# Wider rows for the key and value caches: four heads interleaved on a tile's partitions, in a fused decode kernel

## The chip, the cores and the metric

The kernel runs on one core of a Trainium2 chip. The metric is the device time of one execution in microseconds (us). The time before is 137.99 us, the median of 3 runs (137.91 to 138.05). A profile is one execution taken by the hardware profiler; its span (first to last instruction) is about 2 us shorter than the time.

Engines: PE is TensorE's matmuls, PEld its weight loads, DVE is VectorE, ACT is ScalarE, SPq is the queue of SyncE, which issues the transfers. PSUM is the memory that PE writes its results to. The granted clock is the share of its full speed that TensorE was given at that time, as the profile lists it. L291 means line 291 of that run's kernel; the same statement has another number in another kernel.

## The reference, cut to what matters

One decode step: an attention over the last 4,096 positions of a cache, beside a small GELU MLP, mixed by a sigmoid gate. All data is bf16.

```python
# x (1,1,576); 32 query heads on 16 KV heads of 128; window W = 4096
g = sigmoid((x * gate_w).sum(-1, keepdims=True))
q = x @ wq                                     # wq 576 x 4096
k, v = k_cache[:, :, -4096:], v_cache[:, :, -4096:]   # 16 heads x 4096 x 128, 16 MiB each
p = softmax(q k^T / sqrt(128)) ;  a = (p v) @ wo      # wo 4096 x 576
b = gelu(x @ w1 + b1) @ w2 + b2                # w1 576 x 4608, w2 4608 x 576
out = g * a + (1 - g) * b                      # (1,1,576)
```

Nearly everything is reading: 53.61 MB of weights and cache for one row of output. The scores are so small with these inputs that the attention is close to uniform. A kernel that pairs keys wrongly still passes the comparison.

## The kernel before

The stream of loads is w1, wq, K, V, wo, w2, all issued by SyncE. K and V come one head at a time, each head as 128 rows of 8 KB in one of eight buffers. DVE turns each K tile as 4-byte words (a word is two bf16; the code that follows takes them as turned by 32 x 32 blocks), and PE multiplies it by the query, spread out so that each 32-partition quarter gives its own rows of scores.

```python
k_t = kv_pool.tile([P, NCH * Dh], BF16, name="kv_t", tag="kv")       # 8 buffers, P = 128, NCH = 32
nc.sync.dma_start(out=k_t[:],
    in_=A_k_cache[0, h, Sk - W : Sk, :].rearrange("(p c) d -> p (c d)", p=P))
kt = early[:, (h % 2) * W : (h % 2 + 1) * W]
nc.vector.transpose(out=kt.bitcast(FP32), in_=k_t[:].bitcast(FP32))  # L291
kv = kt.rearrange("p (c b k t) -> p c b k t", c=NCH, b=2, t=2)
for j in range(4):
    for f in range(2):
        nc.tensor.matmul(s_ps[:, f * 512 : (f + 1) * 512].rearrange("p (c k) -> p c k", k=32),
            lhsT=qz[:, h, j, :], rhs=kv[:, f * 16 : (f + 1) * 16, j // 2, :, j % 2], ...)   # L295
# ... softmax: one exp over 128 x 1024; then V, per head, 32 matmuls into o_ps ...
# ... loads: wo in four pieces, then w2 in six ...
for r in range(RO): y_add(ov[:, r : r + 1], wo_t[:, r, :])            # y_add: 512 + 64 columns, one partition
for f in range(NF): y_add(gt[:, f : f + 1], w2_t[:, f, :], stop=(f == NF - 1))
nc.scalar.copy(out=out_row[:, 320:D], in_=y_ps[0:1, 320:D])
nc.vector.tensor_copy(out=out_row[:, 0:320], in_=y_ps[0:1, 0:320])
nc.sync.dma_start(out=out..., in_=out_row[:])
```

Note how PE reads the turned keys: `j % 2` takes every second bf16 of a run of adjacent words.

Of the kernel before, what the change touches and what calls it, by code (L numbers as in the profile page):

```python
# [8 lines left out]
FP32 = mybir.dt.float32  # L9
BF16 = mybir.dt.bfloat16  # L10
ACT = mybir.ActivationFunctionType
ALU = mybir.AluOpType
# [4 lines left out]
def kernel(  # L17
# [21 lines left out]
    NCH = W // P  # L39
# [4 lines left out]
    KM = 4  # L44
    DM = KM * P
    DL = D - DM
    QH = Hq * Dh // 2
    N0 = 512
# [4 lines left out]
    kv_pool = ctx.enter_context(tc.tile_pool(name="kv_pool", bufs=8, side="right"))  # L53
# [7 lines left out]
    x_row = const.tile([1, D], BF16, name="x_row")  # L61
    nc.scalar.dma_start(out=x_row[:], in_=A_x.rearrange("a b d -> (a b) d"))
    gw_row = const.tile([1, D], BF16, name="gw_row")
    nc.scalar.dma_start(out=gw_row[:], in_=gate_w.rearrange("(o n) -> o n", o=1))
    b2_row = const.tile([1, D], BF16, name="b2_row")
    nc.scalar.dma_start(out=b2_row[:], in_=B_b2.rearrange("(o n) -> o n", o=1))
    b1_row = const.tile([1, F], BF16, name="b1_row")
    nc.scalar.dma_start(out=b1_row[:], in_=B_b1.rearrange("(o n) -> o n", o=1))


    w1_t = big.tile([P, KM * F + FH], BF16, name="w1_t", tag="B")
    w1_m = w1_t[:, 0 : KM * F].rearrange("p (k n) -> p k n", k=KM)
    w1_l = w1_t[:, KM * F :]
    w1_src = B_w1[0:DM, :].rearrange("(p k) n -> p k n", k=KM)
    for k in range(KM):
        nc.sync.dma_start(out=w1_m[:, k, :], in_=w1_src[:, k, :])  # L76
    nc.sync.dma_start(out=w1_l, in_=B_w1[DM:D, :].rearrange("r (two n) -> (r two) n", two=2))

    wq_t = big.tile([P, KM * Hq * Dh + QH], BF16, name="wq_t", tag="A")
    wq_m = wq_t[:, 0 : KM * Hq * Dh].rearrange("p (k n) -> p k n", k=KM)  # L80
    wq_l = wq_t[:, KM * Hq * Dh :]
    wq_src = A_wq[0:DM, :].rearrange("(p k) n -> p k n", k=KM)
    for k in range(KM):
        nc.sync.dma_start(out=wq_m[:, k, :], in_=wq_src[:, k, :])
    nc.sync.dma_start(out=wq_l, in_=A_wq[DM:D, :].rearrange("r (two n) -> (r two) n", two=2))
# [4 lines left out]
    one_f = const.tile([1, P], FP32, name="one_f")  # L90
    nc.vector.memset(one_f[:], 1.0)
# [5 lines left out]
    nc.vector.reduce_sum(out=par[:], in_=ident_f[:].rearrange("p (a t) -> p t a", t=2), axis=AX.X)  # L97
    lo32 = const.tile([P, 32], FP32, name="lo32")
# [5 lines left out]
    same = const.tile([P, 4, 32], FP32, name="same")  # L104
    for b in range(4):
        nc.vector.tensor_copy(out=same[:, b, :], in_=lo32[:])

# [7 lines left out]
    early = big.tile([P, 2 * W + 8320], BF16, name="early", tag="C")  # L115
    qz_flat = early[:, 2 * W :]
    qz = qz_flat[:, 0 : Hkv * 4 * P].rearrange("p (h j m) -> p h j m", h=Hkv, j=4)


    xt_ps = ps_m.tile([P, 8], FP32, name="xt_ps", tag="m")  # L120
    for k in range(KM):
        nc.tensor.matmul(
            xt_ps[:, k : k + 1], lhsT=x_row[0:1, k:DM:KM], rhs=one_b[0:1, 0:1], start=True, stop=True
        )
    xd = const.tile([1, DL, 2], BF16, name="xd")
    for t in range(2):
        nc.vector.tensor_copy(out=xd[:, :, t], in_=x_row[0:1, DM:D])
    nc.tensor.matmul(
        xt_ps[:, 4:6],
        lhsT=xd[:].rearrange("p a t -> p (a t)"),  # L130
        rhs=one_b[0:1, 0:2],
        start=True,
        stop=True,
    )
    xt = const.tile([P, KM], BF16, name="xt")
    nc.vector.tensor_copy(out=xt[:], in_=xt_ps[:, 0:KM])
    xl = const.tile([P, 2], BF16, name="xl")
    nc.vector.tensor_tensor(out=xl[:], in0=xt_ps[:, 4:6], in1=par[:], op=ALU.mult)

    nc.vector.memset(qz_flat.bitcast(FP32), 0.0)  # L140

    junk_row = const.tile([1, D], BF16, name="junk_row")
    s0 = const.tile([1, 1], FP32, name="s0")
    nc.vector.tensor_tensor_reduce(
        out=junk_row[:],
        in0=x_row[:],
        in1=gw_row[:],
# [7 lines left out]
    nc.tensor.matmul(g_ps[:, 0:1], lhsT=one_f[0:1, 0:P], rhs=s0[0:1, 0:1], start=True, stop=True)  # L155
# [11 lines left out]
        out=b2g[:], in0=b2_row[:], scalar1=omg[0:1, 0:1], scalar2=None, op0=ALU.mult  # L167
# [3 lines left out]
    y_ps = ps_y.tile([1, 1024], FP32, name="y_ps")  # L171

    def y_add(vec, row, start=False, stop=False):
        nc.tensor.matmul(  # L174
            y_ps[0:1, 0:N0], lhsT=vec, rhs=row[:, 0:N0], start=start, stop=stop, skip_group_check=True
        )
        nc.tensor.matmul(  # L177
            y_ps[0:1, N0:D], lhsT=vec, rhs=row[:, N0:D], start=start, stop=stop, skip_group_check=True
        )

    y_add(one_f[0:1, 0:1], b2g[0:1, :], start=True)
# [3 lines left out]
    for c in range(NF):  # L185
        f0 = (c // NJ) * FH + c % NJ
        nc.tensor.matmul(  # L187
            h_ps[:, c : c + 1],
            lhsT=b1_row[0:1, f0 : (c // NJ + 1) * FH : NJ],
            rhs=one_b[0:1, 0:1],  # L190
            start=(c == 0),
            stop=False,
            skip_group_check=True,
        )
    for k in range(KM):
        for c in range(NF):
            f0 = (c // NJ) * FH + c % NJ
            nc.tensor.matmul(  # L198
                h_ps[:, c : c + 1],
                lhsT=w1_m[:, k, f0 : (c // NJ + 1) * FH : NJ],  # L200
                rhs=xt[:, k : k + 1],
                start=False,
                stop=False,
                skip_group_check=True,
            )
    for j in range(NJ):
        nc.tensor.matmul(  # L207
            h_ps[:, j:NF:NJ],
            lhsT=w1_l[:, j:FH:NJ],
            rhs=xl[:, 0:2],  # L210
            start=False,
            stop=(j == NJ - 1),
            skip_group_check=True,
        )
# [28 lines left out]
    for k in range(KM):  # L243
        for j in range(Hq):
            nc.tensor.matmul(  # L245
                q_ps[:, j : j + 1],
                lhsT=wq_m[:, k, j * Dh : (j + 1) * Dh],
                rhs=xt[:, k : k + 1],
                start=(k == 0 and j == 0),
                stop=False,  # L250
                skip_group_check=True,
            )
    for j in range(Hq // 2):
        nc.tensor.matmul(
            q_ps[:, j : Hq : Hq // 2],
            lhsT=wq_l[:, j * Dh : (j + 1) * Dh],
            rhs=xl[:, 0:2],
            start=False,
            stop=(j == Hq // 2 - 1),
            skip_group_check=True,  # L260
        )
# [11 lines left out]
    for b in range(4):  # L273
        rows = slice(32 * b, 32 * b + 32)
        diag = qz_flat[rows, 32 * b : 32 * b + Hkv * 514].rearrange("p (h m) -> p h m", m=514)
        eng = nc.vector.tensor_copy if b % 2 == 0 else nc.scalar.copy
        eng(
            out=diag[:, :, 0:512].rearrange("p h (j m) -> p h j m", m=P)[:, :, :, 0:2],
            in_=qj_ps[rows].rearrange("p j h t -> p h j t"),
        )  # L280


    s_ps = ps_s.tile([P, NCH * 32], FP32, name="s_ps")
    for h in range(Hkv):
        k_t = kv_pool.tile([P, NCH * Dh], BF16, name="kv_t", tag="kv")
        nc.sync.dma_start(
            out=k_t[:],
            in_=A_k_cache[0, h, Sk - W : Sk, :].rearrange("(p c) d -> p (c d)", p=P),
        )
        kt = early[:, (h % 2) * W : (h % 2 + 1) * W]  # L290
        nc.vector.transpose(out=kt.bitcast(FP32), in_=k_t[:].bitcast(FP32))  # L291
        kv = kt.rearrange("p (c b k t) -> p c b k t", c=NCH, b=2, t=2)
        for j in range(4):
            for f in range(2):
                nc.tensor.matmul(  # L295
                    s_ps[:, f * 512 : (f + 1) * 512].rearrange("p (c k) -> p c k", k=32),
                    lhsT=qz[:, h, j, :],
                    rhs=kv[:, f * 16 : (f + 1) * 16, j // 2, :, j % 2],
                    start=(h == 0 and j == 0),
                    stop=(h == Hkv - 1 and j == 3),  # L300
                    skip_group_check=True,
                )

# [5 lines left out]
    mh = const.tile([1, Hq], FP32, name="mh")  # L309
    nc.vector.reduce_max(out=mh[:], in_=mt_ps[:].rearrange("p (b h) -> p h b", b=4), axis=AX.X)  # L310
    mh4 = const.tile([1, 4, Hq], FP32, name="mh4")
    for b in range(4):
        nc.vector.tensor_copy(out=mh4[:, b, :], in_=mh[:])
# [22 lines left out]


    o_ps = ps_o.tile([P, Hq], FP32, name="o_ps")
    for h in range(Hkv):
        v_t = kv_pool.tile([P, NCH, Dh], BF16, name="kv_t", tag="kv")  # L340
        nc.sync.dma_start(
            out=v_t[:],
# [79 lines left out]
```

## Time and profile before

| what | before |
|---|---|
| time, span | 137.99 us, 136.1 us |
| K transposes on DVE | 16, mean 2,304 ns |
| score matmuls | 128; within a run one starts every 0.217 us (from the starts in the trace, granted clock 1.00) |
| last weight byte landed (from the packets in the trace) | 131.68 us |
| last matmul ended | 133.17 us |

The page of the profile: busy share of DVE, then of the DMA engines (tenths), and the rate moved, in 40 slices of 3.40 us each.

```profile
DVE  5873002228689999989974250000000030000001
...
DMA  4999999999999999999999999999999999999940
GB/s 122 423 425 421 420 419 419 408 420 412 421 421 424 419 417 421 419 417 424 419 421 414 419 421 424 412 421 412 417 421 414 427 427 406 433 417 426 403 182 0
```

The DMA row has no hole: the kernel is bound by its loads, at about 420 GB/s. But DVE's row is at 9 or 8 through the K stage, which is the second limit, close behind.

The groups of instructions (line, engine, operation, output and input with shapes, count, then busy us and mean ns of one, then the idle time just before them and who ended it):

```profile
L295 PE MATMUL s_ps<-early 128*128 128x512 bf16 x128 | 32.6, 401 | 10.5 <-DVE early L291 10.5
L291 DVE STREAM_TRANSPOSE early<-kv_t 128x2048 f32<-128x2048 f32 x16 | 36.6, 2304 | 3.6 <-DMA kv_t<-in_A_k_cache_dram 1.9
```

The chain that ended last, in order of time (start, us, what), only its end:

```profile
86.88 18.95 DMA kv_t<-in_A_v_cache_dram
105.85 22.70 DMA w_t<-in_B_w_dram
...
132.92 0.22 PE y_ps L174
133.13 0.04 PE y_ps L177
133.20 0.37 ACT out_row L389
133.60 0.48 DVE out_row L390
```

The last weights land, PE works off the rows of w2 that are left, and two copies run one after the other.

### The profile page before, as it was taken

How to read it: one execution, taken by the hardware profiler on the slowest of the kernel's cores; microseconds unless marked ns; L12 is line 12 of the kernel's file. 1: busy time of each engine (PE TensorE's matmuls, PEld its weight loads, DVE VectorE, ACT ScalarE, POOL GpSimd, SP SyncE). 2: the span in 40 equal slices, each digit the busy share in tenths (PEclk: the TensorE clock that was granted, in tenths of full speed). 3: DMA queues.
4: the chain of work that ended last, by engine and by line, in shares of the span. 5: the costliest groups of instructions: out<-in, count | busy, mean ns of one | idle time of the engine just before them, and what ended most of it. 6: DMA issues, size and time to landing. Idle time of an engine off the chain costs nothing.

```text
span 136.1 us, 2522 instructions
## 1 busy us (share of the span) xinstructions
PE 90.0 (66%) x1140; PEld 54.9 (40%) x1140; DVE 53.4 (39%) x83; ACT 3.8 (3%) x8; POOL 0.7 (1%) x6
## 2 busy tenths in 40 slices
PE   0099999352997978768774239453352459987891
PEld 0089599341342323323231239452342433433340
DVE  5873002228689999989974250000000030000001
ACT  3000000000000000000000300000000000000001
POOL 2000000000000000000000000000000000000000
PEclk9999999999999999999999655555555555799999
DMA  4999999999999999999999999999999999999940
GB/s 122 423 425 421 420 419 419 408 420 412 421 421 424 419 417 421 419 417 424 419 421 414 419 421 424 412 421 412 417 421 414 427 427 406 433 417 426 403 182 0
DMA packets 7509, 53.79 MB, mean 395 GB/s; under 512 B 837, under 2 KB 841, under 8 KB 1481
## 3 DMA queue, kind: packets, MB, share of 16 engines
q1 hardware_dynamic: 7490, 53.61, 95.6%
q8 instruction: 9, 0.15, 0.4%
q14 instruction: 2, 0.02, 0.0%
q10 hardware_dynamic: 8, 0.01, 0.0%
HBM read 53.62 MB, written 0.00 MB: 394 GB/s over the span
## 4 chain that ended last, share of the span: by engine, by line
DMA 77%; DVE 9%; PE 9%; issue 2%; SPq 1%; ACT 0%; DVEq 0%
DMA kv_t<-in_A_v_cache_dram 27%; DMA kv_t<-in_A_k_cache_dram 27%; DMA w_t<-in_B_w_dram 24%; DVE early L291 9%; PE s_ps L295 5%; PE y_ps L174 3%; PE o_ps L346 1%; SPq L76 1%; PE y_ps L177 0%; DVE out_row L390 0%; ACT out_row L389 0%; DVEq L291 0%
## 5 line engine op out<-in xcount | busy, mean ns | idle before, releaser
L295 PE MATMUL s_ps<-early 128*128 128x512 bf16 x128 | 32.6, 401 | 10.5 <-DVE early L291 10.5
L291 DVE STREAM_TRANSPOSE early<-kv_t 128x2048 f32<-128x2048 f32 x16 | 36.6, 2304 | 3.6 <-DMA kv_t<-in_A_k_cache_dram 1.9
L346 PE MATMUL o_ps<-pt,kv_t 128*128 128x2 bf16 x512 | 15.4, 165 | 16.2 <-DMA kv_t<-in_A_v_cache_dram 13.7
L295 PEld LDWEIGHTS <-early 128*128 128x128 bf16 x128 | 12.8, 100 | 29.9 <-issue 16.3
L346 PEld LDWEIGHTS <-kv_t 128*128 128x128 bf16 x512 | 14.8, 105 | 17.1 <-DMA kv_t<-in_A_v_cache_dram 14.5
L370 DVE COPY o_sb<-o_ps 128x32 f32<-128x32 f32 x1 | 0.2, 191 | 29.1 <-PE o_ps L346 29.1
L174 PE MATMUL y_ps<-wo_t,ov 128*1 128x512 bf16 x32 | 10.9, 471 | 0.6 <-DMA wo_t<-in_A_wo_dram 0.6
L174 PE MATMUL y_ps<-w_t,gt 128*1 128x512 bf16 x36 | 9.2, 379 | 1.8 <-DMA w_t<-in_B_w_dram 1.8
L390 DVE CAST out_row<-y_ps 1x320 bf16<-1x320 f32 x1 | 0.5, 478 | 22.8 <-ACT out_row L389 22.8
L198 PE MATMUL h_ps<-xt,w_t 128*128 128x1 bf16 x144 | 9.3, 201 | 0.0
L198 PEld LDWEIGHTS <-w_t 128*128 128x128 bf16 x144 | 9.1, 167 | 0.2 <-issue 0.2
L177 PE MATMUL y_ps<-wo_t,ov 128*1 128x64 bf16 x32 | 7.0, 218 | 0.0
L177 PE MATMUL y_ps<-w_t,gt 128*1 128x64 bf16 x36 | 6.9, 192 | 0.0
L174 PEld LDWEIGHTS <-ov 128*1 128x1 bf16 x32 | 3.2, 100 | 6.6 <-issue 3.8
L245 PE MATMUL q_ps<-xt,wq_t 128*128 128x1 bf16 x128 | 3.9, 165 | 2.3 <-DMA wq_t<-in_A_wq_dram 2.3
L174 PEld LDWEIGHTS <-gt 128*1 128x1 bf16 x36 | 3.0, 84 | 4.8
L245 PEld LDWEIGHTS <-wq_t 128*128 128x128 bf16 x128 | 3.7, 105 | 2.4 <-DMA wq_t<-in_A_wq_dram 2.4
L216 DVE COPY hacc<-h_ps 128x36 f32<-128x36 f32 x1 | 0.2, 195 | 11.1 <-PE h_ps L207 11.1
L177 PEld LDWEIGHTS <-gt 128*1 128x1 bf16 x36 | 3.0, 84 | 2.1 <-issue 2.1
L140 DVE MEMSET early<- 128x4160 f32 x1 | 3.5, 3525 | 0.8 <-issue 0.8
L177 PEld LDWEIGHTS <-ov 128*1 128x1 bf16 x32 | 3.0, 94 | 0.2 <-issue 0.2
L187 PE MATMUL h_ps<-one_b,b_row 1*128 1x1 bf16 x36 | 2.4, 196 | 0.3 <-DMA b_row<-in_B_b_dram 0.3
(75 smaller groups left out, 31.5 us busy)
## 6 DMA issues: line engine op xcount, KB each, us to landing
kv_t<-in_A_k_cache_dram SPq DMA_DIRECT2D x16, 1024.0 KB, 18.2
kv_t<-in_A_v_cache_dram SPq DMA_DIRECT2D x16, 1024.0 KB, 17.5
w_t<-in_B_w_dram SPq DMA_DIRECT2D x5, 1152.0 KB, 9.0
wo_t<-in_A_wo_dram SPq DMA_DIRECT2D x4, 1152.0 KB, 20.5
wq_t<-in_A_wq_dram SPq DMA_DIRECT2D x4, 1024.0 KB, 13.6
w_t<-in_B_w_dram SPq DMA_DIRECT2D x2, 1296.0 KB
w_t<-in_B_w_dram SPq DMA_DIRECT2D x1, 720.0 KB, 22.0
w_t<-in_B_w_dram SPq DMA_DIRECT2D x1, 576.0 KB
```

The lines of the kernel that those rows point to most:

```text
L76: nc.sync.dma_start(out=w1_m[:, k, :], in_=w1_src[:, k, :])
L140: nc.vector.memset(qz_flat.bitcast(FP32), 0.0)
L174: nc.tensor.matmul(y_ps[0:1, 0:N0], lhsT=vec, rhs=row[:, 0:N0], start=start, stop=stop, skip_group_check=True)
L177: nc.tensor.matmul(y_ps[0:1, N0:D], lhsT=vec, rhs=row[:, N0:D], start=start, stop=stop, skip_group_check=True)
L187: nc.tensor.matmul(h_ps[:, c : c + 1], lhsT=b1_row[0:1, f0 : (c // NJ + 1) * FH : NJ], rhs=one_b[0:1, 0:1], start=(c == 0), stop=False, sk ...
L198: nc.tensor.matmul(h_ps[:, c : c + 1], lhsT=w1_m[:, k, f0 : (c // NJ + 1) * FH : NJ], rhs=xt[:, k : k + 1], start=False, stop=False, skip_ ...
L216: nc.vector.tensor_copy(out=hacc[:], in_=h_ps[:])
L245: nc.tensor.matmul(q_ps[:, j : j + 1], lhsT=wq_m[:, k, j * Dh : (j + 1) * Dh], rhs=xt[:, k : k + 1], start=(k == 0 and j == 0), stop=False ...
L291: nc.vector.transpose(out=kt.bitcast(FP32), in_=k_t[:].bitcast(FP32))
L295: nc.tensor.matmul(s_ps[:, f * 512 : (f + 1) * 512].rearrange("p (c k) -> p c k", k=32), lhsT=qz[:, h, j, :], rhs=kv[:, f * 16 : (f + 1) * ...
L346: nc.tensor.matmul(o_ps[:, 2 * h : 2 * h + 2], lhsT=v_t[:, c, :], rhs=pt[:, c, 2 * h : 2 * h + 2], start=(c == 0), stop=(c == NCH - 1),)
L390: nc.vector.tensor_copy(out=out_row[:, 0:320], in_=y_ps[0:1, 0:320])
```

## The change

Intent: longer pieces per row in the loads, a shorter tail, and less work left when the last weights land.

1. K and V come four heads at a time. Partition 4k + b holds head b, key block k, so a partition's row is 32 KB and a whole group is 4 MB, in one of four large buffers which K, V, w2 and wo share. Loads are of 1 to 4 MB. w1 and wq also come in longer contiguous runs.
2. Because four heads are interleaved on the partitions, the turned words of the four heads are interleaved too. The transpose undoes that while it writes: it writes at a step of 8 words, so that each head's 8 words lie together.
3. The probabilities of the four heads must be kept apart. Each half of the scores is exponentiated four times, with a bias of -1e30 on the rows of the other heads ("masked exp copies").
4. Half of w2 is loaded and used between K and V instead of at the end.
5. The output row y sits on 2 partitions of PSUM (0 and 32, 288 columns each), so one copy replaces two.

```diff
-        nc.vector.transpose(out=kt.bitcast(FP32), in_=k_t[:].bitcast(FP32))
+    # head_rows: cache[0, 4g:4g+4, -W:].rearrange("b (k c) d -> k b (c d)", k=32)
+    for g in range(NG):                                   # 4 groups of 4 heads
+        k_t = big.tile([P, NCK, Dh], BF16, name="k_t", tag="CDBA"[g])
+        load(k_t, A_k_cache, g, k_cuts[g])
+        for f in range(2):
+            for u in range(2):
+                nc.vector.transpose(
+                    out=kt[...].bitcast(FP32).rearrange("p (n b k) -> p n k b", b=HB, k=8),
+                    in_=k_t[...].bitcast(FP32).rearrange("p (n k b) -> p n k b", b=HB, k=8))
+            kv = kt[:].rearrange("p (c e b k t) -> p c e b k t", e=2, b=HB, k=8, t=2)
+            # matmuls as before, rhs=kv[:, :, j // 2, b, :, j % 2]
...
+            nc.scalar.activation(out=p_t[:, cs, :, b], in_=s_ps[...], func=ACT.Exp,
+                bias=negm[:, b : b + 1], scale=SCALE, accum_out=...)      # b in 0..3, two halves
...
+    w2_t = big.tile([P, NF, D], BF16, name="w2_t", tag="B")   # the buffer of K's third group
+    nc.sync.dma_start(out=w2_t[:, 0:NJ, :], in_=w2_src[:, 0])
+    for f in range(NJ):
+        y_add(gt[:, f : f + 1], w2_t[:, f, :])
...
+    for g in range(NG):
+        v_t = big.tile([P, NCK, Dh], BF16, name="v_t", tag="CDAC"[g])   # the last reuses V's first
+        load(v_t, A_v_cache, g, v_cuts[g])
...
+        for s in range(2):                                  # y_add
+            nc.tensor.matmul(y_ps[32 * s : 32 * s + 1, :], lhsT=vec, rhs=row[:, s * DH : (s + 1) * DH], ...)
...
-    nc.scalar.copy(...) ; nc.vector.tensor_copy(...)
+    nc.vector.tensor_copy(out=out_row[0:33, :], in_=y_ps[0:33, :])
```

## The prediction

> **What bounds it now.** The slices show DMA at 0.99 from 2 to 131 us, about 420 GB/s, for 53.61 MB. The chain of waits is 77% DMA; PE is busy 66%, DVE 39%. After the last weight bytes come 36 output matmuls of w2 (0.245 us a row) ending at 133.17, two serial copies (0.36 and 0.48 us) and an output transfer of about 2 us: span 136.1, time 138.0. The K stage is close to a second limit: 16 transposes of 2.30 us against 2.5 us of DMA per MB.
>
> **What the change does.**
> 1. Longer rows. The trace's packets took 313 ns (8,192 B), 351 (9,216), 393 (10,368), 180 (4,608): an estimated 9.6 ns plus 27.0 bytes/ns. Data rows fall from 6,656 to 3,840, so 176 fewer per engine, 1.7 us; 22 fewer completion packets of 9 ns, 0.2 us. All on the critical path: about -1.9 us.
> 2. Tail. One copy of 288 columns replaces two serial ones: -0.4 us. With half of w2 gone from the end, w2's last 18 rows land within 6.3 us of wo's last 20; at 0.245 us a row PE needs 9.3 us and would end 3 us late. [...]
> 3. DVE. Transposes stay 16 x 2,048 fp32, but now write with a step of 8 words. [...]a reduction reading at a step of 32 words took 373 ns, a contiguous one 264, the same shape from PSUM 278: 0.7 to 0.85 ns more per element. For writes nothing here shows it. Estimate with the same penalty: 3.7 to 4.1 us each.
> 4. Middle. Four 4 MB buffers hold all of K; w2's first half waits for the third group's 12 transposes. They start near 30.5 us and K's stream ends near 65, so a transpose up to about 2.9 us is hidden. At 3.8 us w2 is issued near 76 and the queue runs dry for about 11 us. Eight masked exps (about 6 us of ACT instead of 1.1) hide behind w2 and V.
>
> **Sum.** Without the write penalty: -1.9 -0.4 -0.7 = about 135 us. With it: 142 to 150. I hold the unpenalised case somewhat likelier: putting w2 ahead of V would be odd if DVE lagged far.
>
> Predicted 135.8 us, 8 in 10 between 133.3 and 148. Faster by over 2%: 0.36; within 2%: 0.25; slower: 0.39.
>
> **What would show it.** Step 1: 32 KB packets near 1.22 us and slices of 426 to 430 GB/s in V. Step 2: the two y matmuls of a row starting nearly together, PE ending under 1 us after the last weights land. Step 3: mean of the transposes, 2.3 or above 3.5 us. Step 4: a DMA slice below 9 after K, with the SP queue waiting for DVE before w2.
>
> **What would make it wrong.** A write penalty between (3 us); heads 8 MB apart in HBM slowing reads; no column concurrency (+2.5 us); PE clock at 0.5 in the tail (now 0.50 in V).

The sum came to about 135 us: 138.0 less 1.9, 0.4 and 0.7. The ground of the last term, that PE works on the two halves of a row of y at the same time, is cut from step 2 with the term: it was the author's assumption, which no trace showed at that time (e9 and e1 measured it later; it is also what the prediction calls column concurrency). The "about 6 us" of the masked exps is an estimate; the trace of before gives the same with its exp of 1.11 us four times and eight reads of the accumulator at 0.19.

## The result, and the profile after

The changed kernel took 151.3 us (150.46 to 151.7, 4 runs; a run counts as slow when it is over 1.5% above the fastest of its kernel) against 138.01 before: ratio 1.0956, 95% interval 1.0925 to 1.0987. It is slower by 9.6%. Here and below a ratio is the mean time of one kernel's fast runs over that of the kernel before in the same rounds, so it is not quite the ratio of the medians that are quoted.

| what | before | after |
|---|---|---|
| time, span (us) | 138.01, 136.1 | 151.3, 149.5 |
| mean K transpose (ns) | 2,304 | 3,776 |
| last weight byte landed (us) | 131.68 | 144.98 |
| last matmul ended (us) | 133.17 | 146.34 |
| packets of K, V | 8,192 B, 313 ns | up to 32,768 B, 1,213 ns |

The same three rows of the page, in slices of 3.74 us:

```profile
DVE  5990022099999999999999980406350000100001
...
DMA  5999999999999999950089999999963899999940
GB/s 163 428 429 420 434 431 397 421 445 434 425 421 419 421 434 425 408 237 0 0 277 427 444 438 447 438 460 421 430 298 66 377 403 428 451 437 393 404 158 0
```

Two holes have opened in the stream. The first, after K, is two slices at 0 with thin slices beside them; the packets in the trace put it at 67.14 to 75.52 us. The second, at the slices of 298 and 66, has no data from 112.95 to 115.22 us. Where the stream flows it is as fast as hoped. DVE is at 9 from start to end of the K stage.

The groups that answer to those of before, and the new exps:

```profile
L296 DVE STREAM_TRANSPOSE kt<-k_t 128x2048 f32<-128x2048 f32 x16 | 58.3, 3776 | 0.0
L309 PE MATMUL s_ps<-kt,qz_flat 128*128 128x512 bf16 x128 | 38.6, 466 | 26.1 <-DVE kt L296 26.1
...
L347 ACT ACTIVATE p_t<-s_ps,negm 128x512 bf16<-128x512 f32 x8 | 9.7, 1425 | 66.4 <-DVE negm L338 66.4
```

Each transpose moves as many words as before and takes 1.47 us longer. DVE's idle time before them is 0.0: it never waits, so the K stage is now as long as its 16 transposes.

The waits of the DMA queue (who, at which issue, waited for whom: us in total, times, longest):

```profile
SPq L280 <- PE o_ps L391: 20.8, 1, 20.8
...
SPq L363 <- DVE kt L296: 16.8, 1, 16.8
```

L363 is the issue of w2's first half, which takes over the buffer of K's third group and so waits for that group's transposes. L280 is the issue of V's last group, which reuses the buffer of V's first group and so waits until PE has multiplied that one (L391). These are the two holes. The chain that ended last shows the same, from the first transpose to the end:

```profile
30.74 12.30 DVE kt L296 x4
...
67.32 7.22 DVE kt L296 x2
74.54 0.03 DVEq L296
74.58 14.47 DVE kt L296 x4
89.05 0.04 issue
89.09 5.32 PE s_ps L309 x16
...
97.39 3.77 ACT p_t L347 x5
101.16 5.92 ACT p_t L347 x10
107.10 2.31 DVE pt L355
...
110.48 6.82 PE o_ps L391 x256
...
117.70 21.35 DMA wo_t<-in_A_wo_dram
139.05 0.04 issue
139.09 7.25 PE y_ps L178 x68
```

K was in by 67 us, but its transposes end at 89. w2's half is issued near 75 and, with three groups of V, bridges to about 113. The softmax starts 21.5 us later than before (its first exp at 97.39 us against 75.91), so V's first group is multiplied only from 110, and the last group of V comes too late to keep the queue full.

The two copies at the end of before are one here; its line, with the output's issue, from the timeline (start, duration, engine, what, in brackets the idle time before):

```profile
143.84 2.47 PE L178 MATMUL y_ps<-w_t,gt 128*1 128x288 bf16 x36
146.36 0.45 DVE L425 CAST out_row<-y_ps 33x288 bf16<-33x288 f32 x1 [16.40 <-PE y_ps L178]
146.84 0.63 SPq L426 DMA_DIRECT2D out_dram<-out_row  x1
```

36 matmuls of 288 columns, that is 18 rows, took 2.47 us; at the granted clock of 1.00, from 144.04 us on, a row starts every 0.122 us. Before, a row took 0.245 at the same clock.

### The profile page after: what moved, and what is told of

Same layout as the page of the kernel before. It is cut to its first block, busy times and chain, and to the rows that moved or that the text cites. A ratio compares the mean times of both kernels' runs of the same rounds, so it can differ in the third digit from the quotient of the medians.

```text
span 149.5 us, 2460 instructions
## 1 busy us (share of the span) xinstructions
PE 85.1 (57%) x1126; PEld 53.3 (36%) x1126; DVE 78.7 (53%) x81; ACT 11.9 (8%) x21; POOL 0.7 (0%) x6
## 4 chain that ended last, share of the span: by engine, by line
DVE 38%; DMA 33%; PE 15%; ACT 7%; issue 5%; SPq 0%; DVEq 0%; ACTq 0%
DVE kt L296 34%; DMA wo_t<-in_A_wo_dram 14%; DMA wq_t<-in_A_wq_dram 14%; ACT p_t L347 6%; PE y_ps L178 5%; PE o_ps L391 5%; DMA w_t<-in_B_w_dram 4%; PE s_ps L309 4%; DVE pt L355 2%; DVE m L320 1%; PE q_ps L242 1%; PE t_ps L373 0%; DVE qz_flat L265 0%; DVE out_row L425 0%; PE mt_ps L322 0%
## 5 line engine op out<-in xcount | busy, mean ns | idle before, releaser
L296 DVE STREAM_TRANSPOSE kt<-k_t 128x2048 f32<-128x2048 f32 x16 | 58.3, 3776 | 0.0
L309 PE MATMUL s_ps<-kt,qz_flat 128*128 128x512 bf16 x128 | 38.6, 466 | 26.1 <-DVE kt L296 26.1
L309 PEld LDWEIGHTS <-qz_flat 128*128 128x128 bf16 x128 | 14.5, 113 | 49.8 <-issue 39.9
L391 PE MATMUL o_ps<-pt,v_t 128*128 128x8 bf16 x512 | 14.3, 168 | 4.6 <-issue 4.1
L391 PEld LDWEIGHTS <-v_t 128*128 128x128 bf16 x512 | 14.2, 104 | 4.8 <-issue 4.2
L347 ACT ACTIVATE p_t<-s_ps,negm 128x512 bf16<-128x512 f32 x8 | 9.7, 1425 | 66.4 <-DVE negm L338 66.4
L178 PE MATMUL y_ps<-wo_t,ov 128*1 128x288 bf16 x64 | 8.0, 443 | 6.3 <-DMA wo_t<-in_A_wo_dram 6.3
L204 PEld LDWEIGHTS <-w_t 128*128 128x128 bf16 x162 | 10.2, 165 | 1.0 <-issue 1.0
L204 PE MATMUL h_ps<-x,w_t 128*128 128x2 bf16 x162 | 10.4, 202 | 0.0
L355 DVE STREAM_TRANSPOSE pt<-p_t 128x2048 bf16<-128x2048 bf16 x2 | 4.6, 2311 | 7.4 <-ACT p_t L347 7.4
L178 PE MATMUL y_ps<-w_t,gt 128*1 128x288 bf16 x72 | 5.3, 289 | 0.0
```

The lines of the kernel that those rows point to most:

```text
L178: nc.tensor.matmul(y_ps[32 * s : 32 * s + 1, :], lhsT=vec, rhs=row[:, s * DH : (s + 1) * DH], start=start, stop=stop, skip_group_check=True,)
L204: nc.tensor.matmul(h_ps[:, j:NF:NJ], lhsT=w1_t[:, i, j:FH:NJ], rhs=x2[:, i, :], start=False, stop=(i == NI - 1 and j == NJ - 1), skip_grou ...
L296: nc.vector.transpose(out=kt[:, u * half : (u + 1) * half] .bitcast(FP32) .rearrange("p (n b k) -> p n k b", b=HB, k=8), in_=k_t[:, c0 : c ...
L347: nc.scalar.activation(out=p_t[:, cs, :, b], in_=s_ps[:, f * 512 : (f + 1) * 512].rearrange("p (c k) -> p c k", k=8), func=ACT.Exp, bias=n ...
L355: nc.vector.transpose(out=pt[:, cs, :].rearrange("p c h -> p (c h)"), in_=p_t[:, cs, :, :].rearrange("p c k b -> p (c k b)"),)
L391: nc.tensor.matmul(o_ps[:, 8 * g : 8 * g + 8, 0], lhsT=v_t[:, c, :], rhs=pt[:, c, 8 * g : 8 * g + 8], start=(c == 0), stop=(c == NCK - 1),)
```

## The experiments

**Theories.** A: the whole loss is the write step of the transposes; the stream stalls as a consequence. B: heads that lie 8 MB apart, or 32 KB packets, slow the reads. C: the order of loads (half of w2 ahead of V) or the eight exps starve the queue, whatever DVE does. (The expectations use B and C for rivals of their own, which each of them spells out. Where they speak of a line or of values per line, 16 adjacent bytes are meant, and no more is claimed than what e6 and then e4, e10 and e7 measured; their two column groups are the halves of a row of y, which go to output partitions 0 and 32.) Twelve kernels ran; all agreed with the reference within tolerance, for what that is worth here. A kernel with three or five rounds is timed against the kernel before on the same chip.

### e1_flat_write: the changed kernel, but the transposes write in order

The keys end up paired with the wrong head's queries, so the result is wrong; every instruction keeps its size.

```diff
-    out=kt[...].bitcast(FP32).rearrange("p (n b k) -> p n k b", b=HB, k=8),
-    in_=k_t[...].bitcast(FP32).rearrange("p (n k b) -> p n k b", b=HB, k=8),
+    out=kt[...].bitcast(FP32),
+    in_=k_t[...].bitcast(FP32),
```

> The changed kernel, with one edit: the 16 transposes of K write their columns in order instead of with a step of 8 words (wrong result on purpose; every transfer, matmul and copy stays as it is). Theory A (the write step slows the transposes, and the two dry stretches of the DMA stream follow from it): the transposes fall from 3.64 to 2.30 us, the third group is done near 58 us, w2 is issued before K's stream ends near 66, V's last group waits for nothing, and the time is 134 to 136 us. Rival B (four buffers of 4 MB are too coarse, whatever DVE does): transposes 2.30, but the stream still runs dry by 5 us or more, time above 142. Rival C (the transposes are slow for another cause, such as transfers into the same tile or four heads on a tile): they stay at 3.6 us and the time at 151.

Measured: 135.81 us (135.46 to 136.5), ratio 0.9846 (0.9813 to 0.9878). Its transposes among the groups:

```profile
L296 DVE STREAM_TRANSPOSE kt<-k_t 128x2048 f32<-128x2048 f32 x16 | 36.0, 2290 | 4.9 <-DMA k_t<-in_A_k_cache_dram 4.7
```

The DMA share and rate on its page, in slices of 3.34 us:

```profile
DMA  4999999999999999999999999999999999999950
GB/s 129 432 431 426 432 432 414 407 417 453 421 431 417 434 412 431 431 416 412 446 453 429 451 431 417 421 451 431 421 416 407 402 409 436 431 427 404 411 206 0
```

The transposes are back at 2.29 us, both holes are gone, the stream ends at 129.81 us. With B or C the time would have stayed up: both fall as the cause of the loss. The order of loads and the exps are the same here and cost nothing as long as DVE keeps up. The write step is worth 15.5 us.

### e3_before_step8: the kernel before, with the write step put in

Wrong pairing.

```diff
-        nc.vector.transpose(out=kt.bitcast(FP32), in_=k_t[:].bitcast(FP32))
+        nc.vector.transpose(out=kt.bitcast(FP32).rearrange("p (n b k) -> p n k b", b=4, k=8),
+                            in_=k_t[:].bitcast(FP32).rearrange("p (n k b) -> p n k b", b=4, k=8))
```

> The kernel before, with one edit: its 16 transposes write with a step of 8 words as those of the change do (wrong result on purpose). Theory A: transposes 3.64 instead of 2.30 us, K's last one ends near 89 us instead of 71, V's ninth head waits for the softmax, the stream runs dry for about 10 us, and the time is 150 to 157 us. Rival C (the step costs nothing in itself, the new tile layout does): transposes 2.30, time 138.

Measured: 153.23 us (153.1 to 153.59), ratio 1.1106 (1.1084 to 1.1128). Its transposes among the groups:

```profile
L291 DVE STREAM_TRANSPOSE early<-kv_t 128x2048 f32<-128x2048 f32 x16 | 58.4, 3779 | 0.4 <-DMA kv_t<-in_A_k_cache_dram 0.4
```

So the step alone, with 8 KB rows and the old order, costs as much: 15.2 us. Together with e1 this shows it from both sides.

### e6_write_steps: what a transpose costs by its access pattern

The changed kernel, with a different pattern for each of eight transposes, twice over. Its output is wrong, which doesn't matter for the time.

```diff
+                pat = (4 * g + 2 * f + u) % 8
+                if pat == 0: nc.vector.transpose(out=dst, in_=srcw)
+                elif pat == 1: ... dst "p (n a s) -> p n s a", s=2      # and s=4, 8, 16
+                ... pairs of words hopping 16; hop of 512 words; step 8 on the read side
```

> The changed kernel with eight patterns for its 16 transposes, two of each (wrong result on purpose): written in order, with steps of 2, 4, 8 and 16 words, in pairs that hop 16 words, with a step of 8 words on the read side, and with a hop of 512 words every element. Theory A[...]: in order, step 2 and pairs 2.3 us; [...]the read step about 3.7. If only the one step of 8 is bad[...], the others stay at 2.3.

(Theory A's band for steps of 4, 8, 16 and 512 words put all four among the slow ones.)

Measured: 145.26 us in its single look, with ten of the sixteen transposes penalised; each mean is of two, of 2,048 words per partition:

| pattern | line | ns |
|---|---|---|
| in order | L300 | 2,282 |
| write step 2 words | L302 | 2,282 |
| write pairs of words, hopping 16 | L310 | 2,258 |
| write step 4 | L304 | 3,780 |
| write step 8 | L306 | 3,768 |
| write step 16 | L308 | 3,584 |
| write, hop of 512 words every word | L314 | 3,622 |
| read step 8, write in order | L312 | 3,748 |

Three of these groups as the profile has them:

```profile
L304 DVE STREAM_TRANSPOSE kt<-k_t 128x2048 f32<-128x2048 f32 x2 | 7.6, 3780 | 2.6 <-DMA k_t<-in_A_k_cache_dram 2.6
...
L302 DVE STREAM_TRANSPOSE kt<-k_t 128x2048 f32<-128x2048 f32 x2 | 4.6, 2282 | 0.1
L310 DVE STREAM_TRANSPOSE kt<-k_t 128x2048 f32<-128x2048 f32 x2 | 4.5, 2258 | 0.0
```

The penalty is one step, not a slope: each jump tried from 4 words up (4, 8, 16, 512) costs 1.3 to 1.5 us, 1.75 to 1.85 ns a word in all instead of 1.1, and the jump of 8 does so on the read side (3,748 ns) as well as on the write side (3,768); a jump of 2, or pairs of adjacent words that hop 16, costs nothing (2,282 and 2,258 ns against 2,282 in order). Counted by 16 bytes, all eight rows fit: in order, at a step of 2 or in pairs, at least two words fall into the same 16 bytes, and from a step of 4 up only one. That is a reading of these eight rows; what causes it no run here shows.

### e2_v_first: two groups of V ahead of w2's half

Right result.

```diff
+    for g in range(2):                       # V's first two groups, in the buffers of K's first two
+        v_t = big.tile([P, NCK, Dh], BF16, name="v_t", tag="CD"[g])
+        load(v_t, A_v_cache, g, v_cuts[g])
     w2_t = big.tile([P, NF, D], BF16, name="w2_t", tag="B")
     nc.sync.dma_start(out=w2_t[:, 0:NJ, :], in_=w2_src[:, 0])
```

> The changed kernel with the first two groups of V issued ahead of the first half of w2, so that nothing behind K waits for the third group's transposes. Theory A says that DVE's pace sets when the softmax is done (109 us) and so when V's last group may start (115 us), and that this wait takes up what the first one gives back: the dry stretch after K (about 9 us) goes, the one before V's last group grows from about 4 to about 12 us, and the time stays at 151 within 1. The rival (the place of w2 in the queue is the fault) says 141 to 143 us.

Measured: 147.7 us (146.8 to 148.46), ratio 1.0682 (1.0621 to 1.0743). My 151 was missed by 3 us. The rate on its page, in slices of 3.66 us:

```profile
GB/s 167 423 427 420 420 446 403 412 448 421 430 426 423 426 430 426 405 482 443 439 430 430 430 370 473 420 430 220 0 0 49 394 417 433 431 440 400 410 205 0
```

The chain that ended last, around the issue of V's last group:

```profile
108.99 0.59 PE o_ps L397 x17
109.58 0.47 PE t_ps L366 x2
110.05 1.25 PE o_ps L397 x47
111.32 0.54 SPq L280
111.85 0.05 issue
111.90 10.77 DMA v_t<-in_A_v_cache_dram
```

The first hole is gone, but the second is now 10.2 us long, where the two together had 10.7: V's last group still waits for the softmax, which ends with DVE. So this reordering does not remove the second hole, as theory A has it. What I had not foreseen is that the scheduler, with w2's rows placed later in the program, put matmuls of V's first group ahead of the last step of the softmax. That group was done earlier, and the first packet of V's last group came at 112.65 us instead of 115.22. The order of loads, with the change of schedule that came with it, is thus worth 3.6 us of the 13. In e1, with the order as changed, there is no hole that it could fill.

### e4_pairs: the transposes write pairs of words

Right result. Within a group, the heads 2g and 2g + 1 share pairs: layout (pair of heads, key, head of the pair). DVE writes two adjacent words, then hops.

```diff
-    .rearrange("p (n b k) -> p n k b", b=HB, k=8),                 # out
+    .rearrange("p (n g k s) -> p n k g s", g=2, k=8, s=2),
...
-    rhs=kv[:, :, j // 2, b, :, j % 2],
+    rhs=kv[:, :, j // 2, b // 2, :, b % 2, j % 2],
```

> The changed kernel, with the transposed tile laid out so that two heads' words lie side by side: DVE writes runs of two words and then hops 16, and the score matmuls read every fourth bf16 (8 bytes) instead of every second (right result). Theory A[...]: transposes 2.3 to 2.4 us, no dry stretch, 134 to 136 us if PE reads at 8 bytes as fast as at 4 (0.23 us from matmul to matmul[...]); if PE pays for it, up to 0.45 us a matmul, PE bound in K, 140 to 150. If pairs do not help, transposes stay at 3.6 us and the time at 151.

Measured: 147.99 us (147.2 to 148.14), ratio 1.071 (1.0678 to 1.0743). The groups:

```profile
L309 PE MATMUL s_ps<-kt,qz_flat 128*128 128x512 bf16 x128 | 55.5, 607 | 5.8 <-DVE kt L296 5.8
L296 DVE STREAM_TRANSPOSE kt<-k_t 128x2048 f32<-128x2048 f32 x16 | 36.2, 2295 | 14.9 <-PE s_ps L309 11.7 <-DMA k_t<-in_A_k_cache_dram 3.1
```

The transposes are cured, yet DVE now waits 11.7 us for PE. The timeline shows 47 score matmuls in 20.43 us, one every 0.430 us from start to start, where the changed kernel, within a run of 16 at the same clock, starts one every 0.217. The granted TensorE clock was 1.00 in all of this stretch, so it is not the clock. PE now reads every fourth bf16 instead of every second.

### e10_word_pairs and e7_pe_reads_16B: what PE pays for its operand's step

e10, right result: the layout is (pair of keys, head, key of the pair), which DVE writes at a step of 2 words and PE reads as 2 adjacent words, then a hop of 32 bytes. e7, right result: the transposes write in order and PE picks its head itself, at every eighth bf16.

```diff
+    .rearrange("p (m b l) -> p m l b", b=HB, l=2),                  # e10, out
+    rhs=kv[:, :, j // 2, :, b, :, j % 2],                           # e10, "p (c e m b l t) -> p c e m b l t"
...
+    kv = kt[:].rearrange("p (c e k b t) -> p c e b k t", ...)       # e7; out and in_ in order
```

> The changed kernel with the transposed words laid out as (key pair, head, key of the pair): DVE, for which the head runs fastest, then writes with a step of 2 words[...] and hops only every second word, and the score matmuls read two words of a head side by side, then hop 32 bytes (right result, transfers as in the change). Transposes 2.3 us, as step 2 was in the run of eight patterns. If PE needs two values in 8 bytes, matmuls stay 0.23 us apart and the time is 135 to 136.5 (ratio 0.985). If PE needs four values in a line of 16 bytes, they take 0.43 us as with the reads at 8 bytes, and the time is 147 to 149.

> The changed kernel with transposes written in order and the score matmuls reading every eighth bf16 (16 bytes; right result). Transposes 2.3 us; matmuls at least as slow as with a step of 8 bytes (0.43 us), so a time of 147 or more; if the cost goes on growing with the step, up to 0.85 us a matmul and 190 us.

Measured: e10 took 148.24 us (147.46 to 148.79), ratio 1.0747 (1.0723 to 1.0771); 48 score matmuls in 20.90 us, one every 0.430; its transposes took 2,296 ns. e7 took 202.28 us in a single look, 12 above the most that I had expected; 25 in 21.64 us, one every 0.858.

| kernel | bf16 used per 16 bytes | us from start to start of 512 columns, granted clock 1.00 |
|---|---|---|
| y's matmuls of 512 adjacent columns in e9, below | 8 | 0.217 |
| after (within a run of 16), e1 | 4 | 0.217 |
| e4 (every fourth) | 2 | 0.430 |
| e10 (two, then hop) | 2 | 0.430 |
| e7 (every eighth) | 1 | 0.858 |

From four of eight down, the time goes with the number of 16-byte pieces that the streamed operand touches, about 1.7 ns each (an estimate from these rows), and not with the shape of the step: e4 and e10 differ in their runs and cost the same. Above that nothing is gained: with all eight used, 512 columns still take 0.217 us. At a step of 4 bf16, with two used in each 16 bytes, PE is already at half rate (0.430). The conflict is plain now: of the patterns tried, DVE was at full rate with two words or more per 16 bytes on its side (2,258 to 2,296 ns a transpose), PE with four bf16 of one head or more per 16 bytes (0.217 us a matmul), and four heads interleaved word by word gave each simple layout tried only one of the two.

### e5_row_pairs: adjacent rows of one head on adjacent partitions

Right result. Pairs of words of one head can be had at the source: partition (pair of rows, head, row of the pair). That makes each load two transfers, each over every second partition.

```diff
-    return src.rearrange("b (k c) d -> k b (c d)", k=NKP)
+    return src.rearrange("b (m r c) d -> m r b (c d)", m=NKP // 2, r=2)
...
+    for r in range(2):
+        nc.sync.dma_start(out=tile_[r:P:2, c0 : c0 + n, :]..., in_=src[:, r, :, ...])
```

> The changed kernel, with the partitions of a K or V tile ordered (row pair, head, row of the pair), each load split into two transfers over every second partition. The transposes then write runs of two adjacent words before they hop 8, and the score matmuls read every second bf16 as in the change (right result). Theory A: transposes 2.3 us, matmuls 0.23 us apart, no dry stretch, 134.5 to 137 us, so faster than the kernel before by 1 to 2%. If transfers over every second partition are slower, the stream falls below 400 GB/s in K and V and the time is above 138.

Measured: 205.64 us (202.19 to 207.27), ratio 1.4784 (1.4714 to 1.4855); the profiled run counts as slow, being 2% above the fastest of its six. DVE and PE were both at full rate (2,282 ns a transpose), but the stream was not. The rate on its page, in slices of 5.11 us:

```profile
GB/s 225 433 428 435 411 260 276 237 221 241 223 241 231 237 241 231 241 244 299 397 238 212 234 205 218 225 215 205 225 218 221 189 234 231 256 298 434 404 310 8
```

And its exps among the groups:

```profile
L348 ACT ACTIVATE p_t<-s_ps,negm 128x512 bf16<-128x512 f32 x8 | 5.5, 720 | 83.9 <-DVE negm L339 83.9
```

K and V come mostly at 205 to 245 GB/s, while w1, wq and the last weights keep about 430; a 32 KB packet takes 2,429 ns (median) instead of 1,213. Why these transfers run at half rate no run here tells apart, so it stays open. They write every second partition, but each also reads only every second 32 KB block of a head, and the two were not separated. A side result: the exps, which here write two adjacent bf16 at a time, take 720 ns instead of 1,425 for the same 512 columns of the same input tile, so the doubling in the changed kernel goes with its write at single bf16 with a step of 8 bytes.

### e8_short_rows: what the long rows are worth

e1 with K and V in 8 KB rows, as 32 loads of 1 MB; wrong as e1.

```diff
-    k_cuts = ((32, 32, 64), (64, 64), (64, 64), (64, 32, 32))
+    k_cuts = ((32,) * 4,) * NG
...
-    v_cuts = ((NCK,), (NCK,), (NCK,), (64, 32, 32))
+    v_cuts = ((32,) * 4,) * NG
```

> The kernel with transposes written in order (its time 135.81), with K and V loaded in 8 KB rows again, 32 transfers of 1 MB instead of 16 of 1 to 4 MB (wrong result on purpose, as there). 128 packets more per engine at 9.6 ns and 22 completion packets at 9 ns: the stream ends about 1.4 us later, time 137.2 (ratio to before 0.994). If the rows are worth nothing, 135.8; if the rows are the whole gain, 138.

Measured: 137.49 us (137.17 to 138.42), ratio 0.9975 (0.9951 to 1.0). The stream ends at 131.29 us, 1.48 later than in e1. The long rows of K and V are real and worth about 1.5 us; the packets' times had said so before any run.

### e9_y_one and e11_before_y2: the tail

e9 is e1 with y on one partition (512 + 64 columns, two copies). e11 is the kernel before with y on two partitions and one copy (right result).

```diff
-    y_ps = ps_y.tile([1, 1024], FP32, name="y_ps")                  # e11; e9 is the reverse, on e1
+    y_ps = ps_y.tile([64, DH], FP32, name="y_ps")
+    ... two matmuls of 288 columns, on partitions 0 and 32; one copy of 33 x 288
```

> The kernel with transposes written in order (135.81), with the output sum on one partition again (512 + 64 columns, two serial copies; attention still with wrongly paired keys). If the two column groups run at the same time, undoing it makes the last 38 rows serial: [...]behind the landing of wo at 123.9 us, PE ends near 134.5 instead of 130.6, and with the second copy the time is 139.5 to 141. If the groups do not overlap, only the copy changes: 136.2.

(Its estimate for the 38 rows used what the trace of before shows: a row of y starts every 0.245 us at a granted clock of 1.00, from 117.2 us on, and every 0.48 us at 0.50, from 111.6 to 116.4 us.)

> The kernel before with one part of the change alone: the output sum on two partitions, in two column groups of 288, and one copy. PE's rows fall from 0.245 to about 0.13 us, so the last 18 rows of w2 no longer lag behind the stream's end (131.7): PE ends near 132.1 instead of 133.2, and the copies take 0.45 instead of 0.9 us. Expected 136.3 to 136.8 us (ratio 0.988 to 0.991). If the groups do not overlap, 137.6.

Measured: e9 138.44 us (138.25 to 139.84), ratio 1.0056 (1.002 to 1.0091), 2.6 us above e1, where I had expected 3.7 to 5.2. e11 137.5 us (137.38 to 138.05), ratio 0.9974 (0.9959 to 0.9988), only 0.4 below the kernel before where I had expected 1.1 to 1.6.

In e9 a row takes 0.245 us from start to start, and PE ends 3.6 us after the last weight byte (133.6 against 130.01). In e1, at the same granted clock of 1.00, a row takes 0.122, its two matmuls start 5 ns apart, and PE ends 0.75 after. So the two halves of y do run side by side when they go to different output partitions, here 0 and 32: 0.245 against 0.122 us a row, 2.0x. In the new order of loads this and the single copy are worth 2.6 us; there, half of w2 has gone from the end and the rows of wo and w2 come close together.

In the old order PE had less to catch up, 1.49 us, and e11 gained little even of that, for two reasons that its trace shows. The first is the granted clock. It was 0.50 from 130.42 us on, and the last ten rows came one every 0.240 us instead of 0.122, so PE ended at 132.98 us and not near 132.1 as I had expected; in the kernel before, the clock was 1.00 from 117.1 us to the end. What lowered it no run here tells, though the mean clock of each of e11's six runs (0.79 to 0.82) is below that of the kernel before (0.85 to 0.86). The second is the output. The end of e11's timeline:

```profile
133.03 0.45 DVE L394 CAST out_row<-y_ps 33x288 bf16<-33x288 f32 x1 [22.20 <-PE y_ps L177]
133.50 0.62 SPq L395 DMA_DIRECT2D out_dram<-out_row  x1
```

The output is issued at 133.50 instead of 134.10 us. But its issue takes 0.62 us and not the 0.32 of before, and so in every kernel with y on two partitions (0.62 to 0.64 us in eleven traces, 0.31 to 0.33 in three with one row). From the start of the issue to the end of the span it takes 2.54 us instead of 2.00 (2.54 to 2.81 in the traces with two rows, 2.00 to 2.13 in those with one). The transfer now has two rows, and gives nearly all of the 0.6 us back. I had counted neither.

### e12_head_pairs: a version that satisfies both

Right result by construction. DVE writes pairs as in e4; PE streams both heads of a pair in one matmul, 16 adjacent words. That makes as many matmuls as before, each with the queries of both heads. The scores of the wrong head fall into columns which the exps leave out (they read every second column of a score tile twice as wide), and rows which the mask sets aside already.

```diff
-    rhs=kv[:, :, j // 2, b // 2, :, b % 2, j % 2],                            # e4
+    rhs=kv[:, q * SL // 2 : (q + 1) * SL // 2, j // 2, gg, :, j % 2],         # k = 16: (key, head of pair)
+    lhsT=qz[:, hp, j, :]                                                      # 4 query columns, not 2
...
-    in_=s_ps[:, f * 512 : (f + 1) * 512].rearrange("p (c k) -> p c k", k=8),
+    in_=s_ps[:, f * 1024 : (f + 1) * 1024].rearrange("p (c k s) -> p c k s", k=8, s=2)[:, :, :, b % 2],
```

> Right result by construction. The transposes write pairs of adjacent words (key tile layout: head pair, key, head of the pair), and the score matmuls stream both heads of a pair at once, 16 adjacent words[...]; the row products of the wrong head land in rows and columns that the masked exps and a wider score tile (2,048 columns) set aside. Theory (the loss is the write step of the transposes, and the moving operand costs by the 16-byte lines that it touches): transposes about 2.3 us, score matmuls about 0.23 us apart, no dry stretch of the queue, 135.0 to 136.5 us, ratio 0.98 to 0.99, so ahead of both kernels. If the matmuls cost by their step and not by lines: they stay at 0.43 us apart and the time near 148. If the wider softmax (maximum over 2,048 columns, exps that read every second PSUM word) is not hidden behind w2: a dry stretch before V's last group and 138 to 141.

Measured: 136.48 us (135.66 to 136.81, 6 runs), ratio 0.9878 (0.9854 to 0.9901). Its groups:

```profile
L310 PE MATMUL s_ps<-kt,qz_flat 128*128 128x512 bf16 x128 | 30.8, 391 | 14.4 <-DVE kt L295 14.4
L295 DVE STREAM_TRANSPOSE kt<-k_t 128x2048 f32<-128x2048 f32 x16 | 36.0, 2291 | 4.9 <-DMA k_t<-in_A_k_cache_dram 4.7
...
L321 DVE TENSOR_REDUCE m<-s_ps 128x1 f32<-128x2048 f32 x1 | 2.3, 2292 | 3.5 <-PE s_ps L310 3.5
```

Both engines are at full rate, 16 matmuls take 3.63 us (one starts every 0.217), the DMA row of its page is 9 without a hole, and the last byte lands at 130.05 us, 0.24 after e1's. The maximum over a tile twice as wide takes 2.29 us instead of 1.23 and is hidden. The exps took 1,421 ns where the changed kernel's took 1,425, so reading every second fp32 of the scores added nothing to that. It beats the changed kernel by 15 us and the kernel before by 1.2%. It also supports the reading of e4, e7 and e10: the transposes write just as in e4, and on PE's side the count and size of the matmuls are the same while each touches half as many 16-byte pieces.

## Why the prediction was wrong

The prediction was 135.8 us with a range up to 148; the result is 151.3.

- **What bounds the kernel before** was right: loads at 420 GB/s, with DVE's transposes close behind.
- **Step 1, longer rows (-1.9 us)** was right. 32 KB packets took 1,213 ns (predicted 1.22 us), e1's stream ends 1.87 us earlier than before, and e8 puts 1.48 of it on K and V. The fears of slow reads from heads 8 MB apart did not come true. The prediction's test of even slices at 426 to 430 GB/s in V was poor: with packets this long the slices scatter (391 to 469 in e12).
- **Step 2, the tail (-0.4 and -0.7)** was right for both terms where DVE kept up, though the second had rested on an assumption. In e1 PE ends 0.75 us after the last byte instead of 1.49, and one copy of 0.45 us replaces 0.84. In the changed kernel itself PE ended 1.36 us after, with the granted clock at 0.50 until 144.04 us and a row every 0.24 us. The fear of "+2.5 us" if the halves of y did not run side by side is close to what e9 measured, +2.6 with the second copy in it. The missed term is the output's transfer from two partitions: 2.67 us from the start of its issue to the end of the span in e1, against 2.00 before. Together, the unpenalised sum of "about 135 us" stands against 135.81 in e1.
- **Step 3 is the step that failed:** "I hold the unpenalised case somewhat likelier: putting w2 ahead of V would be odd if DVE lagged far." The estimate itself ("3.7 to 4.1 us each") was right, 3.776 measured, and the strided reduction in the profile of before (373 ns against 264 and 278) had been its measured ground. I then set it aside by guessing at intent from the order of loads, which is no measurement. e1, e3 and e6 show in its place that each write step tried from 4 words up (4, 8, 16 and 512) costs 1.3 to 1.5 us a transpose, and that this one thing is the whole loss.
- **Step 4 was right in mechanism and too small.** The first hole came where it was said: w2 was issued near 75 and the queue was dry for 8.4 us, with thin slices at its edges ("about 11 us"). But "Eight masked exps (about 6 us of ACT instead of 1.1) hide behind w2 and V" failed when DVE was late. They took 9.7 us (97.39 to 107.10), since each writes single bf16 at a step and takes 1.4 us, and with the late softmax they held back V's first group, its buffer and V's last load: the second hole. So even the penalised range, up to 150, ended short of 151.3. Against e1, the stream ends 15.2 us later: 8.4 for the first hole, 2.3 with no data at all in the second, and the rest in the slices beside them, where only some engines had work.

## What to carry to other kernels

When a layout is changed so that loads get longer rows, look at who undoes the interleaving, and cost its access pattern at every engine that touches it: here 1.9 us of DMA were bought with 1.5 us on each of 16 transposes, in a stage where DVE had almost no slack. If an estimate from the profile says that an engine falls behind, do not discard it because the code looks as if its author knew better; put the doubtful instruction's penalty in the centre of the prediction. When the pattern must stay, choose one in which both the writer and the reader use enough of every 16 bytes (in these runs pairs of words for DVE, 2,258 ns a transpose, and four bf16 for PE, 0.217 us a matmul), even if PE then computes products that are thrown away.
